# Strassen's scheme for the first product of the last two token chunks of a dense MLP

## The chip, the core and the metric

One core of a Trainium2 chip runs the whole program as one launch. The metric is the device time of one execution, in microseconds. The engines are TensorE (PE, matmuls), VectorE (DVE), ScalarE (ACT), GpSimd (POOL) and SyncE (SP, whose queue issues nearly all transfers). Each engine takes its instructions in the order in which they stand on it.

## What is computed

The program is a chain of three stages on 4 batches of 544 tokens: local attention with global tokens, a gated MLP with a convolution, and this last stage, with its input `x` of 2176 x 512:

```
X = fft over tokens, then over features, real part
u = x + X
un = (u - mean) / sqrt(var + 1e-6)          over the 512 features
out = u + relu(un @ w_ch1) @ w_ch2          w_ch1: 512 x 2048, w_ch2: 2048 x 512
```

All products are made to nearly float32 accuracy: each operand is split in a high and a low part, and `mm3` issues three matmuls (low x high, high x low, high x high) for each 128 x 128 block of weights.

## The kernel before

Features lie on the 128 partitions, tokens on the free axis. The last stage works on five chunks of tokens (`NT = 436`, the last has 432); a chunk's `u` is kept in device memory (`u_d`) and fetched by `load_uc(c)` (L940) into `uc`, as four blocks of 128 features. `ln(c)` (L949) is a generator that makes mean and variance in small steps: VectorE or GpSimd adds the feature blocks, the sum is split in two parts (`sr`), two matmuls with `ones` give the mean in a PSUM bank (L968), VectorE subtracts it (L971), and the centred chunk is stored as high and low parts `chl`. The variance follows in the same way (L987), and its reciprocal root `rs` scales the result at the end.

The hidden layer has 16 blocks of 128. A step `v` of the loop at L1103 stands for one pair (chunk, block): `c_g1(v)` (L998) issues 12 matmuls of `ch1[m]` on `chl` into a bank (`g1` or `pv`), ScalarE takes the relu as the high part and VectorE the low part (`hd`, L1011, L1012), and two steps later `c_g2(v-2)` (L1022) issues 12 matmuls of `ch2[m]` on `hd` into four banks `a0` to `a3`. `plan` (L995) holds 80 steps: chunks 0 and 1 take blocks 0 to 7 and then 8 to 15, then chunks 2, 3 and 4 take all 16 blocks each. So steps 24 to 31 are chunk 1 on blocks 8 to 15, steps 32 to 47 are chunk 2, 48 to 63 chunk 3, and 64 to 79 chunk 4. At a chunk's end VectorE multiplies by `rs` (L1044), adds `uc` (L1047), and SP sends four pieces to `out` (L1049). The last two steps are interleaved by feature block, and the last block is cut in halves (L1032 to L1038).

The weights come as 64-bit floats. `make_c` (L931) turns a block into float32 and splits it, with two value buffers `mags` that are used in turn; blocks 8 to 15 are made by `make_c` in steps 9 to 16 of the program, and some blocks are made earlier, stored in device memory as `kept` and loaded back. PE and SP run strictly in the order of the program text (`manual_schedule`); the order on VectorE, ScalarE and GpSimd is set by a scheduler from priorities. At step 26 the program issues `load_uc(2)`, and at step 27 it starts `ln(2)`, whose mean is due on PE ahead of the first matmuls of step 30:

```
if v in (26, 36, 52):
    load_uc({26: 2, 36: 3, 52: 4}[v])
if v in (1, 27, 36, 52):
    lnq.append(ln({1: 1, 27: 2, 36: 3, 52: 4}[v]))
step(lnq)
c_g1(v)
c_g2(v - 2)
```

Of the kernel before, what the change touches and what calls it, by code (L numbers as in the profile page):

```python
# [151 lines left out]
def fused_kernel(ctx: ExitStack, tc: tile.TileContext, d, out):  # L152
    nc = tc.nc
    pe, act, dve, gp, sp = nc.tensor, nc.scalar, nc.vector, nc.gpsimd, nc.sync
# [780 lines left out]
    ln_t, uc_t, rs_t, cft = {}, {}, {}, []  # L935

    def width(c):
        return min(NT, B * S - NT * c)

    def load_uc(c):  # L940
        t = uc_t[c] = up.tile([128, 5, NT], F32, tag="u", name="uc")
        a, z = NT * c, NT * c + width(c)
# [72 lines left out]
    def c_mm(v, e, a=0, z=None):  # L1015
# [4 lines left out]
        mm3(acc[e][:, a:z], w[:, 0, f], w[:, 1, f], hd[:, 0, a:z], hd[:, 1, a:z], m in one[:2], m in one[2:] and z in (None, width(c)))  # L1020

    def c_g2(v):  # L1022
        end = len(plan) - 2
# [8 lines left out]
        cuts = [(e, 0, n) for e in range(4)]  # L1032
        if v > end:
            cuts[3:] = [(3, 0, h), (3, h, n)]
        for x in cuts:
            if v > end:
                c_mm(end, *x)
            c_mm(v, *x)  # L1038
        if m == 15 or c < 2 and m == 7:
# [2 lines left out]
            for es in [[x] for x in cuts] if v > end else [cuts]:
                for e, a, z in es:
                    dve.tensor_mul(tmp[:, e, a:z], acc[e][:, a:z], rs_t[c][:, a:z])  # L1044
                for e, a, z in es:
                    o = uc[:, e, a:z]
                    dve.tensor_add(o, o, tmp[:, e, a:z])  # L1047
                    if m == 15:
                        sp.dma_start(out[128 * e:128 * e + 128, NT * c + a:NT * c + z], o)  # L1049
# [122 lines left out]
```

## Time and profile before

| | |
|---|---|
| median of three runs | 788.04 us (787.4 to 788.87) |
| the profiled execution | 789.74 us, its span 787.8 us |
| PE busy | 762.4 us, 97% of the span |
| DVE, ACT, POOL busy | 476.9 us, 369.4 us, 167.4 us |
| chain that ended last | PE 78%, DVE 9%, ACT 8%, DMA 2% |

The span runs from the first to the last recorded instruction or transfer of one execution. Steps 0 to 79 of the last stage fill roughly its second half. A busy share is an average over the stages; the chain of waits names, for each moment, the engine on which the end of the program hangs.

### The profile page before, as it was taken

Reading aid. Unit: us, or ns where it says so; the run is one execution under the profiler, and the core shown is the slowest. Engines: PE = TensorE matmul, PEld = TensorE weight load, DVE = VectorE, ACT = ScalarE, POOL = GpSimd, SP = SyncE. Lnnn points to the kernel's source line nnn. Section 1 sums busy time; section 2 is a strip of 40 time slices with the busy share of each in tenths; the row PEclk is TensorE's granted clock in tenths of the full one; section 3 lists DMA queues with packets and bytes.
Section 4 is the critical chain, followed back from the end, with each engine's and each line's share of the span. In section 5 each row is a group of like instructions: output and inputs, shape, how many; then the busy total and the mean of one; then the engine's idle time right before and its main releaser. Section 6 shows DMA issues by size and latency. Waiting matters only on the chain.

```text
span 787.8 us, 13621 instructions
## 1 busy us (share of the span) xinstructions
PE 762.4 (97%) x5278; PEld 701.6 (89%) x5278; DVE 476.9 (61%) x1134; ACT 369.4 (47%) x936; POOL 167.4 (21%) x216
## 2 busy tenths in 40 slices
PE   5898999999999999999999999999999999999997
PEld 4577889998999899998898999999999999999997
DVE  5999977778777878699865778435422132213113
ACT  6988777767777785544442474213131112111110
POOL 3764322323332332000430022100121013000000
PEclk9999999999999999999999999999999999999999
DMA  8754221452337133456430750020200020001001
GB/s 309 268 181 168 85 83 54 162 187 83 102 134 247 56 111 117 112 183 201 146 103 1 275 208 1 1 92 0 92 1 1 1 90 1 1 1 45 1 1 46
DMA packets 37088, 77.80 MB, mean 99 GB/s; under 512 B 3784, under 2 KB 22216, under 8 KB 37024
## 3 DMA queue, kind: packets, MB, share of 16 engines
q1 hardware_dynamic: 36432, 74.52, 27.2%
q0 software_dynamic: 592, 2.42, 1.3%
q8 instruction: 42, 0.69, 0.4%
q14 instruction: 22, 0.18, 0.1%
HBM read 61.72 MB, written 15.20 MB: 98 GB/s over the span
## 4 chain that ended last, share of the span: by engine, by line
PE 78%; DVE 9%; ACT 8%; DMA 2%; issue 1%; POOL 0%; SPq 0%; DVEq 0%; ACTq 0%; POOLq 0%
PE ps_a L169 33%; PE ps_g L169 21%; PE ps_pv L169 15%; PE ps_s L169 5%; PE ps_t L169 3%; ACT pb L346 3%; DVE y L561 1%; DVE mag L659 1%; DVE pb L336 1%; DMA raw_w<-in_w_out_dram 1%; DMA mask<-in_mask_dram 1%; DVE w_w L676 1%; DVE mag L664 1%; ACT h L544 1%; DVE g L581 1%
## 5 line engine op out<-in xcount | busy, mean ns | idle before, releaser
L169 PE MATMUL ps_a<-g,w_w 128*128 128x254 f32 (+1 forms) x768 | 113.5, 295 | 1.3 <-DVE g L581 0.9
L169 PE MATMUL ps_g<-x,w_w 128*128 128x256 f32 (+1 forms) x768 | 111.4, 294 | 3.3 <-ACT h L544 2.1
L169 PEld LDWEIGHTS ps_g<-x,w_w 128*128 128x128 f32 x768 | 100.2, 188 | 10.0 <-ACT h L544 3.7
L169 PEld LDWEIGHTS ps_a<-g,w_w 128*128 128x128 f32 x768 | 101.0, 190 | 6.2 <-issue 3.8
L359 POOL TENSOR_SCALAR pb<-pb,sm 128x224 f32<-128x224 f32 x128 | 85.6, 685 | 83.2 <-DVE sm L354 80.0
L169 PE MATMUL ps_a<-hd,w_w 128*128 128x436 f32 (+1 forms) x480 | 101.4, 360 | 0.0
L169 PEld LDWEIGHTS ps_a<-hd,w_w 128*128 128x128 f32 x480 | 90.1, 188 | 4.8
L561 DVE SCALAR_TENSOR_TENSOR y<-h,convw,y 128x254 f32<-128x254 f32 (+1 forms) x128 | 69.1, 541 | 16.3 <-ACT y L557 15.3
L1012 DVE SCALAR_TENSOR_TENSOR hd<-ps_pv,hd 128x436 fp32r<-128x436 f32 (+1 forms) x40 | 24.2, 604 | 86.9 <-ACT hd L1011 86.9
L169 PE MATMUL ps_a<-hd,w_v 128*128 128x436 f32 (+1 forms) x360 | 76.2, 360 | 0.0
L1011 ACT ACTIVATE hd<-ps_pv 128x436 fp32r<-128x436 f32 (+1 forms) x40 | 21.4, 534 | 111.3 <-PE ps_pv L169 111.3
L1012 DVE SCALAR_TENSOR_TENSOR hd<-ps_g,hd 128x436 fp32r<-128x436 f32 (+1 forms) x40 | 24.3, 607 | 81.2 <-ACT hd L1011 81.2
L1011 ACT ACTIVATE hd<-ps_g 128x436 fp32r<-128x436 f32 (+1 forms) x40 | 21.4, 535 | 110.3 <-PE ps_g L169 110.3
L191 POOL TENSOR_SCALAR mag<-mag 128x512 f32<-128x512 f32 x32 | 26.9, 840 | 208.5 <-ACT mag L190 208.4
L169 PEld LDWEIGHTS ps_a<-hd,w_v 128*128 128x128 f32 x360 | 67.6, 188 | 3.7
L346 ACT ACTIVATE pb<-pb,sm 128x224 f32<-128x224 f32 x128 | 60.4, 473 | 10.7 <-DVE sm L336 10.4
L169 PE MATMUL ps_g<-chl,w_w 128*128 128x436 f32 (+1 forms) x240 | 51.0, 361 | 0.0
L169 PE MATMUL ps_pv<-chl,w_v 128*128 128x436 f32 (+1 forms) x240 | 50.9, 360 | 0.0
L169 PE MATMUL ps_pv<-chl,w_w 128*128 128x436 f32 (+1 forms) x240 | 50.7, 360 | 0.0
L169 PEld LDWEIGHTS ps_pv<-chl,w_v 128*128 128x128 f32 x240 | 45.1, 188 | 2.5
L169 PEld LDWEIGHTS ps_g<-chl,w_w 128*128 128x128 f32 x240 | 44.8, 188 | 2.7 <-issue 0.3
L169 PEld LDWEIGHTS ps_pv<-chl,w_w 128*128 128x128 f32 x240 | 44.9, 188 | 2.5
(224 smaller groups left out, 1388.7 us busy)
## 6 DMA issues: line engine op xcount, KB each, us to landing
v<-in_v_dram SPq DMA_DIRECT2D x16, 640.0 KB, 4.9
qk<-in_qk_dram SPq DMA_DIRECT2D x16, 464.0 KB, 4.8
raw_r<-in_ch_dram SPq DMA_DIRECT2D x14, 512.0 KB, 5.9
raw_v<-in_ch_dram SPq DMA_DIRECT2D x13, 512.0 KB, 9.1
kept<-w_o SPq DMA_DIRECT2D x12, 512.0 KB, 3.5
w_w<-kept SPq DMA_DIRECT2D x12, 512.0 KB, 4.0
qk<-in_qk_dram SPq DMA_DIRECT2D x16, 304.0 KB, 6.1
u_d<-u SPq DMA_DIRECT2D x4, 1088.0 KB, 5.2
```

Source lines behind the costliest of these rows:

```text
L169: return pe.matmul(o, a, b, start=start, stop=stop)
L191: (clamp or dve).tensor_scalar(mag, mag, TOP, 2.0, op0=ALU.min, op1=ALU.max)
L336: dve.tensor_tensor_reduce(out=pb_of(i, k), in0=sb[k // 2][:, k % 2], in1=mask[:, 2 * where(i)[1] + k % 2], scale=-0.125, scalar=3.0e38, o ...
L346: last_exp[0] = act.activation(p, p, AF.Exp, bias=sm[:, k:k + 1], scale=-1.0, accum_out=sm[:, 4 + k:5 + k])
L359: gp.tensor_scalar(pb_of(i, k), pb_of(i, k), sm[:, 12 + k:13 + k], 1.0, op0=ALU.mult, op1=ALU.mult)
L544: act.activation(hbuf[u % NHB][:, h0:h0 + n], h_bank.pop(u), AF.Relu, scale=0.5)
L561: dve.scalar_tensor_tensor(y, o, convw2[:, m, x:x + 1], y, op0=ALU.mult, op1=ALU.add)
L581: dve.tensor_sub(gate[u][:, 1], y, f32(gate[u][:, 0]))
L659: dve.scalar_tensor_tensor(val, val, 3, tail, op0=ALU.logical_shift_left, op1=ALU.bitwise_or)
L664: dve.scalar_tensor_tensor(val, head, -(2**31), val, op0=ALU.bitwise_and, op1=ALU.bitwise_or)
L1011: act.activation(hd[:, 0], o, AF.Relu)
L1012: dve.scalar_tensor_tensor(hd[:, 1], o, 0.0, f32(hd[:, 0]), op0=ALU.max, op1=ALU.subtract)
```

## The change

Chunks 3 and 4 become 434 tokens wide each and are treated as the two columns of a 2 x 2 block product. For `q` from 0 to 7, the rows are blocks `q` and `q + 8` of `w_ch1`, and the inner dimension is cut in two halves of 256 features. Seven products, in the variant with common sums, replace eight: `a11 b11`, `s2 t2`, `s1 t1`, `s3 t3`, `a12 b21`, `s4 b22`, `a22 t4` (`pair`, L1182 of the changed file). A product is 6 matmuls (two slices of 128 features, three each). VectorE adds the products up in SBUF; block `q` and block `q + 8` of chunk 3 go on to the second product at once, the 16 blocks of chunk 4 (`late`) are kept and get their second product at the end.

The sums of the weights (`s1` to `s4`) are made by `s_make(q)` in steps 17, 19, ... 31: VectorE forms them in the two buffers `mags`, SP stores both in device memory (`sval`), and the next `s_make` may overwrite them when the stores have landed. Eight blocks `ch1[8]` to `ch1[15]` are stored as `kept` in steps 9 to 16. In `pair`, `s_load(q + 1)` fetches the sums into `mags` and the plain weights into `aw`, and `s_split` splits the sums into slots `w0` and `w1`. The sums of the activations (`t1` to `t4`) and all seven operands are made in `pair_norm`, a generator on VectorE and ScalarE in steps 36 to 47, normalized before the product; the operands take the slots of `ch1[2]` to `ch1[15]`. The other steps of the program, with their order on PE, are as before.

```diff
--- before.py
+++ after.py
...
 NT = 436
+WIDE = [436, 436, 436, 434, 434]
...
     def width(c):
...
+        return WIDE[c]
...
-    plan += [(c, m) for c in range(2, 5) for m in range(16)]
+    plan += [(2, m) for m in range(16)]
...
     def c_g2(v):
...
-        h = n // 2
-        cuts = [(e, 0, n) for e in range(4)]
-        if v > end:
-            cuts[3:] = [(3, 0, h), (3, h, n)]
-        for x in cuts:
-            if v > end:
-                c_mm(end, *x)
-            c_mm(v, *x)
+        for e in range(4):
+            c_mm(v, e)
...
+    def s_make(q):
+        v0, v1 = mags
+        for v, w in ((v0, ch1[q]), (v1, ch1[q + 8])):
+            dve.tensor_add(v, f32(w[:, 0]), f32(w[:, 1]))
+        a11, a12, a21, a22 = [x[:, y:y + 256] for x in (v0, v1) for y in (0, 256)]
+        dve.tensor_add(a22, a21, a22)
+        dve.tensor_sub(a21, a11, a21)
+        dve.tensor_sub(a11, a22, a11)
+        dve.tensor_sub(a12, a12, a11)
+        for k in range(2):
+            sval[q, k] = dram.tile([128, 512], F32, name=f"sval{q}_{k}")
+            sp.dma_start(sval[q, k], (v0, v1)[k])
+
+    def s_load(q):
+        if q < 8:
+            for k in range(2):
+                sp.dma_start(mags[k], sval[q, k])
+            t = up.tile([128, 3, 512], F32R, tag="u", name="aw")
+            sp.dma_start(f32(t[:, 0:2]), kept[q])
+            sp.dma_start(f32(t[:, 2]).rearrange("p (a b) -> p a b", a=2), kept[q + 8][:, :, 256:512])
+            a_hl[q] = t
+
+    @prio("cv")
+    def s_split(q):
+        if q < 8:
+            s_hl[q] = [put(wp, f"w{k}", mags[k]) for k in range(2)]
...
+    def pair_norm():
+        x = xp.tile([128, 8, NW], F32, tag="x", name="xx")
+        two["x"] = [x[:, 4 * j:4 * j + 4] for j in range(2)]
+        for j in range(2):
+            load_uc(3 + j, two["x"][j])
+        yield
+        yield
+        two["sr"] = up.tile([128, 5, NT], F32R, tag="u", name="xsr")[:, 0:2, 0:NW]
+        x_sum(0)
...
+        t_split("t4", b11)
...
+    def out_add(c, e, o, a=0, z=NW):
+        u = uc_t[c][:, e, a:z]
+        dve.tensor_add(u, u, o)
+        t0 = sum(WIDE[:c])
+        sp.dma_start(out[128 * e:128 * e + 128, t0 + a:t0 + z], u)
...
+        for q in range(8):
+            s_load(q + 1)
+            aw, (s24, s13) = a_hl.pop(q), s_hl.pop(q)
+            wa = {"a11": aw[:, 0:2, 0:256], "a12": aw[:, 0:2, 256:512], "a22": aw[:, 2].rearrange("p (a b) -> p a b", a=2)}
+            for s_, nm in ((s24, "s2 s4"), (s13, "s3 s1")):
+                for k, n_ in enumerate(nm.split()):
+                    wa[n_] = s_[:, :, 256 * k:256 * k + 256]
+
+            def prod(w, x):
+                o = bank(next(four))[:, 0:NW]
+                for k in range(2):
+                    f = slice(128 * k, 128 * k + 128)
+                    mm3(o, wa[w][:, 0, f], wa[w][:, 1, f], t_hl[x][k][:, 0], t_hl[x][k][:, 1], k == 0, k == 1)
+                return o
+
+            x = prod("a11", "b11")
+            with pri("cev"):
+                act.copy(p1, x)
+            if q == 0:
+                c_g2(len(plan) - 1)
+            x = prod("s2", "t2")
+            with pri("cev"):
+                dve.tensor_add(u2, p1, x)
+            x = prod("s1", "t1")
+            with pri("cev"):
+                dve.tensor_add(w5, u2, x)
+            x = prod("s3", "t3")
+            with pri("cev"):
+                dve.tensor_add(late[q + 8], w5, x)
+                dve.tensor_add(u2, u2, x)
+            if q:
+                g2(accs, q + 7, hds.pop(q + 7))
+            x = prod("a12", "b21")
+            with pri("cev"):
+                dve.tensor_add(p1, p1, x)
+            high_low(q, p1)
+            x = prod("s4", "b22")
+            with pri("cev"):
+                dve.tensor_add(late[q], w5, x)
+            s_split(q + 1)
+            x = prod("a22", "t4")
+            with pri("cev"):
+                dve.tensor_add(c21, u2, x)
+            high_low(q + 8, c21)
+            g2(accs, q, hds.pop(q))
+            if q in (5, 7):
+                load_uc(3 if q == 5 else 4)
+        order = [x for q in range(8) for x in (q, q + 8)]
+        high_low(0, late[0])
+        g2(accs, 15, hds.pop(15))
+        for e in range(4):
+            out_add(3, e, accs[e])
+        accs = [bank(next(four))[:, 0:NW] for _ in range(4)]
+        high_low(8, late[8])
+        for k, m in enumerate(order[:14]):
+            if k + 2 < 16:
+                high_low(order[k + 2], late[order[k + 2]])
+            g2(accs, m, hds.pop(m))
+        for e in range(4):
+            for m in order[14:]:
+                g2(accs, m, hds[m], [e])
+            out_add(4, e, accs[e])
...
-        if v in (26, 36, 52):
-            load_uc({26: 2, 36: 3, 52: 4}[v])
-        if v in (1, 27, 36, 52):
-            lnq.append(ln({1: 1, 27: 2, 36: 3, 52: 4}[v]))
+        if 9 <= v < 17:
+            x = TAIL[2 * v - 18]
+            kept[x] = dram.tile([128, 2, 512], F32, name=f"kept{x}")
+            sp.dma_start(kept[x], f32(ch1[x]))
+        if 17 <= v < 33 and v % 2:
+            s_make((v - 17) // 2)
+        if v == 26:
+            load_uc(2)
+        if v in (1, 27):
+            lnq.append(ln({1: 1, 27: 2}[v]))
+        if v == 32:
+            T_SLOTS += [(wp, f"w{m}") for m in range(2, 8)] + [(vp, f"v{m}") for m in range(8, 15)] + [(rb, "r1")]
+            lnq.append(pair_norm())
+        if v == 44:
+            s_load(0)
+        if v == 46:
+            s_split(0)
         step(lnq)
         c_g1(v)
         c_g2(v - 2)
+    c_g2(len(plan) - 2)
+    while lnq:
+        step(lnq)
+    pair()
...
```

Three places in the order of instructions. On SP, at step 25 (end of chunk 0), before:

```order
L205 DMA raw_r_5640<-in_ch_dram 128x1024
L205 DMA raw_r_5642<-in_ch_dram 128x4x256
L205 DMA raw_o<-in_ch_dram 128x1024
L1049 DMA out_dram<-uc 128x436 x4
L946 DMA uc<-u_d_4977 128x4x216
L946 DMA uc<-u_d_5215 128x4x220
```

And now (`mag_5101`, `mag_5102` are the two value buffers; each pair of `sval` rows is one `s_make`, and the first two pairs here are the fourth and the fifth):

```order
L1063 DMA sval_0_6247<-mag_5101 128x512
L1063 DMA sval_1_6249<-mag_5102 128x512
L1063 DMA sval_0_6313<-mag_5101 128x512
L1063 DMA sval_1_6315<-mag_5102 128x512
L1045 DMA out_dram<-uc 128x436 x4
L950 DMA uc<-u_d_4977 128x4x216
L950 DMA uc<-u_d_5215 128x4x220
L1063 DMA sval_0_6398<-mag_5101 128x512
L1063 DMA sval_1_6400<-mag_5102 128x512
```

Between the last load of raw weights and the four stores of chunk 0's result there now stand the stores of eight weight blocks and of five `s_make`s; the two loads of chunk 2's `uc` are behind all of them.

On VectorE, where `ln(2)` makes its sum, before (L958 to L961 are the sum, L971 the subtraction of the mean, `hd` rows belong to steps 26, 27, 28 and 29):

```order
L1012 SCALAR_TENSOR_TENSOR hd<-ps_pv,hd 128x436
L1012 SCALAR_TENSOR_TENSOR hd<-ps_g_6331,hd 128x436
L958 TENSOR_TENSOR cf<-uc 128x872
L959 TENSOR_TENSOR cf<-cf 128x436
L961 TENSOR_TENSOR chl<-cf,chl 128x436
L1012 SCALAR_TENSOR_TENSOR hd<-ps_pv,hd 128x436
L1012 SCALAR_TENSOR_TENSOR hd<-ps_g_6387,hd 128x436
L971 TENSOR_TENSOR cf<-uc,ps_t 128x872 x2
```

And now, starting behind the `hd` row of step 29 (L1055 to L1060 are an `s_make`, here the sixth and half of the seventh; L962, L963 and L965 are the same sum of `ln(2)`):

```order
L1055 TENSOR_TENSOR mag_5101<-w_w_4817 128x512
L1055 TENSOR_TENSOR mag_5102<-w_v_5898 128x512
L1057 TENSOR_TENSOR mag_5102<-mag_5102 128x256
L1058 TENSOR_TENSOR mag_5102<-mag_5101,mag_5102 128x256
L1059 TENSOR_TENSOR mag_5101<-mag_5102,mag_5101 128x256
L1060 TENSOR_TENSOR mag_5101<-mag_5101 128x256
L962 TENSOR_TENSOR cf<-uc 128x872
L1055 TENSOR_TENSOR mag_5101<-w_w_4882 128x512
L963 TENSOR_TENSOR cf<-cf 128x436
L1055 TENSOR_TENSOR mag_5102<-w_v_5944 128x512
L1057 TENSOR_TENSOR mag_5102<-mag_5102 128x256
L965 TENSOR_TENSOR chl<-cf,chl 128x436
```

The sum of `ln(2)` stood ahead of the `hd` rows of steps 28 and 29; now it stands behind both, behind the whole sixth `s_make`, and with three operations of the seventh inside it. The fifth `s_make` stands between the `hd` rows of steps 28 and 29.

On VectorE at the end of chunk 2, before:

```order
L1044 TENSOR_TENSOR cf<-ps_a_6570,uc 128x436
L1012 SCALAR_TENSOR_TENSOR hd<-ps_g_7011,hd 128x436
L1044 TENSOR_TENSOR cf<-ps_a_6571,uc 128x436
L1047 TENSOR_TENSOR uc<-uc,cf 128x436
L1044 TENSOR_TENSOR cf<-ps_a_6572,uc 128x436
L1044 TENSOR_TENSOR cf<-ps_a_6573,uc 128x436
L1047 TENSOR_TENSOR uc<-uc,cf 128x436 x3
```

And now, from the last of chunk 2's adds on (L1227 to L1244 add up the first seven products, L228 are the splits of the next weight sums, L1200 makes the low parts of the first two hidden blocks):

```order
L1043 TENSOR_TENSOR uc<-uc,cf 128x436
L1227 TENSOR_TENSOR hh<-hh,ps_g_7220 128x434
L1230 TENSOR_TENSOR hh<-hh,ps_pv 128x434
L1231 TENSOR_TENSOR hh<-hh,ps_pv 128x434
L228 TENSOR_TENSOR w_w_7259<-mag_5102,w_w_7259 128x512
L1236 TENSOR_TENSOR hh<-hh,ps_s 128x434
L1240 TENSOR_TENSOR hh<-hh,ps_t 128x434
L228 TENSOR_TENSOR w_w_7256<-mag_5101,w_w_7256 128x512
L1244 TENSOR_TENSOR hh<-hh,ps_g_7262 128x434
L1200 SCALAR_TENSOR_TENSOR hd<-hh,hd 128x434 x2
```

For `q = 0` the low part of the first hidden block stands behind the sum of the seventh product; for `q` from 1 to 7 it stands ahead of it.

## Rows read from the trace of the kernel before

**Rows 1.** The page: busy time by engine; granted clock in 40 slices.

```profile
PE 762.4 (97%) x5278; PEld 701.6 (89%) x5278; DVE 476.9 (61%) x1134; ACT 369.4 (47%) x936; POOL 167.4 (21%) x216
...
PEclk9999999999999999999999999999999999999999
```

**Rows 2.** Chain of waits, steps 51 and 77: start us, length us, what.

```profile
640.25 2.38 PE ps_g L169 x12
...
764.23 2.35 PE ps_g L169 x12
```

**Rows 3.** Timeline at the end: start us, length us, engine, instructions.

```profile
781.74 0.48 PE L169 MATMUL ps_a<-hd,w_r 128*128 128x216 f32 x3
...
783.26 0.67 DVE L1044 TENSOR_TENSOR cf<-ps_a,uc 128x216 f32<-128x216 f32 x2
783.85 0.67 DVE L1047 TENSOR_TENSOR uc<-uc,cf 128x216 f32<-128x216 f32 x2
```

**Rows 4.** DMA issues: KB each, median us to landing.

```profile
kept<-w_o SPq DMA_DIRECT2D x12, 512.0 KB, 3.5
w_w<-kept SPq DMA_DIRECT2D x12, 512.0 KB, 4.0
out_dram<-uc SPq DMA_DIRECT2D x16, 218.0 KB, 2.0
out_dram<-uc SPq DMA_DIRECT2D x2, 108.0 KB, 1.7
```

**Rows 5.** Chain of waits, steps 27 to 30.

```profile
526.76 2.37 PE ps_a L169 x12
...
531.52 2.37 PE ps_a L169 x12
...
536.28 2.39 PE ps_a L169 x12
538.67 0.40 PE ps_t L169 x2
```

**Rows 6.** Timelines of DVE and of SP's queue around the end of chunk 0.

```profile
504.06 0.68 DVE L227 TENSOR_TENSOR w_o<-mag,w_o 128x512 fp32r<-128x512 f32 x1
...
520.04 2.94 SPq L1049 DMA_DIRECT2D out_dram<-uc  x4
525.24 1.20 SPq L946 DMA_DIRECT2D uc<-u_d  x2
527.36 0.61 DVE L1012 SCALAR_TENSOR_TENSOR hd<-ps_g,hd 128x436 fp32r<-128x436 f32 x1 [4.16 <-ACT hd L1011]
531.86 1.07 DVE L958 TENSOR_TENSOR cf<-uc 128x872 f32<-128x872 f32 x1 [3.89 <-DMA uc<-u_d]
534.20 0.61 DVE L961 TENSOR_TENSOR chl<-cf,chl 128x436 fp32r<-128x436 f32 x1 [0.62 <-ACT chl L960]
```

**Rows 7.** Groups on DVE by shape: busy us, mean ns.

```profile
L227 DVE TENSOR_TENSOR w_v<-mag,w_v 128x512 fp32r<-128x512 f32 x13 | 9.0, 691 | 6.0 <-ACT w_v L226 6.0
L873 DVE TENSOR_TENSOR ab<-ps_t,ab 92x256 fp32r<-92x256 f32 x5 | 2.1, 419 | 3.6 <-ACT ab L872 3.6
L1047 DVE TENSOR_TENSOR uc<-uc,cf 128x436 f32<-128x436 f32 x24 | 13.7, 604 | 0.0
```

**Rows 8.** Windows after the last matmul: us, five busy times, granted clock, DMA.

```profile
785.00:786.00 1.00, 0.00 (x0) 0.00 (x0) 0.00 (x0) 0.00 (x0) 0.00 (x0) 0.90 0.65 220
786.00:787.00 1.00, 0.00 (x0) 0.00 (x0) 0.00 (x0) 0.00 (x0) 0.00 (x0) 0.50 0.01 2
```

**Rows 9.** Timeline of PE near the start: transposes of one shape, 128 x 128.

```profile
12.84 0.42 PE L375 MATMUL ps_a<-ident,pb 128*128 128x128 f32 x1
13.05 0.42 PE L376 MATMUL ps_a<-ident,pb 128*128 128x128 f32 x1
...
17.91 0.27 PE L375 MATMUL ps_s<-ident,pb 128*128 128x128 f32 x1
18.02 0.27 PE L376 MATMUL ps_s<-ident,pb 128*128 128x128 f32 x1
```

More of the change, by code (lines that the diff above doesn't have):

```diff
@@ L937, in width, with load_uc @@
     def width(c):
[L938 to L942, printed above, removed]
+        return WIDE[c]
+    def load_uc(c, dst=None):
+        if dst is None:
+            uc_t[c] = up.tile([128, 5, NT], F32, tag="u", name="uc")
+            dst = uc_t[c][:, 0:4]
+        a0 = a = sum(WIDE[:c])
+        z = a0 + width(c)
         while a < z:
@@ L945, in load_uc @@
             n = min(z - a, S - o)
-            sp.dma_start(t[:, 0:4, a - NT * c:a - NT * c + n], u_d[b][:, :, o:o + n])
+            sp.dma_start(dst[:, :, a - a0:a - a0 + n], u_d[b][:, :, o:o + n])
             a += n
@@ L1013, in c_g1, with c_mm @@
         hid[v] = hd
-    def c_mm(v, e, a=0, z=None):
+    def c_mm(v, e):
         c, m = plan[v]
@@ L1019, in c_mm @@
         f = slice(128 * e, 128 * e + 128)
-        mm3(acc[e][:, a:z], w[:, 0, f], w[:, 1, f], hd[:, 0, a:z], hd[:, 1, a:z], m in one[:2], m in one[2:] and z in (None, width(c)))
+        mm3(acc[e], w[:, 0, f], w[:, 1, f], hd[:, 0], hd[:, 1], m in one[:2], m in one[2:])
     def c_g2(v):
-        end = len(plan) - 2
-        if not 0 <= v < len(plan) or v == end:
+        if not 0 <= v < len(plan):
             return
@@ L1041, in c_g2 @@
             tmp = cft[0][:, 0:4, 0:n]
[L1042 to L1049, printed above, removed]
+            for e in range(4):
+                dve.tensor_mul(tmp[:, e], acc[e], rs_t[c])
@@ new lines, in c_g2 @@
+            for e in range(4):
+                o = uc[:, e, 0:n]
+                dve.tensor_add(o, o, tmp[:, e])
+                if m == 15:
+                    sp.dma_start(out[128 * e:128 * e + 128, NT * c:NT * c + n], o)
+    NW = WIDE[3]
+    T_SLOTS = []
+    T_ORDER = ("b11", "b21", "t2", "t1", "t3", "b22", "t4")
+    sval, two, t_hl, s_hl, a_hl = {}, {}, {}, {}, {}
+    def s_make(q):
[10 more added lines that the diff above has]
+            sp.dma_start(sval[q, k], (v0, v1)[k])
@@ new lines, in s_load, with x_sum @@
+    def s_load(q):
[10 more added lines that the diff above has]
+            s_hl[q] = [put(wp, f"w{k}", mags[k]) for k in range(2)]
+    def x_sum(j):
+        cf = cft[0]
+        x, sr = two["x"][j], two["sr"]
+        dve.tensor_add(cf[:, 0:2, 0:NW], x[:, 0:2], x[:, 2:4])
+        dve.tensor_add(cf[:, 0, 0:NW], cf[:, 0, 0:NW], cf[:, 1, 0:NW])
+        act.copy(sr[:, 0], cf[:, 0, 0:NW])
+        dve.tensor_sub(sr[:, 1], cf[:, 0, 0:NW], f32(sr[:, 0]))
@@ new lines, in x_mean, with x_center, x_square @@
+    def x_mean(o):
+        sr = two["sr"]
+        mm(o, ones, sr[:, 1], True, False)
+        mm(o, ones, sr[:, 0], False, True)
+        return o
+    def x_center(j):
+        mu = x_mean(fbank()[:, 0:NW])
+        for k in (slice(0, 2), slice(2, 4)):
+            x = two["x"][j][:, k]
+            dve.tensor_sub(x, x, mu[:, None, :].to_broadcast([128, 2, NW]))
+    def x_square(j):
+        cf, sr = cft[0], two["sr"]
+        for k in (slice(0, 2), slice(2, 4)):
+            act.activation(cf[:, k, 0:NW], two["x"][j][:, k], AF.Square)
+        dve.tensor_add(cf[:, 0:2, 0:NW], cf[:, 0:2, 0:NW], cf[:, 2:4, 0:NW])
+        dve.tensor_add(cf[:, 0, 0:NW], cf[:, 0, 0:NW], cf[:, 1, 0:NW])
+        act.copy(sr[:, 0], cf[:, 0, 0:NW])
+        dve.tensor_sub(sr[:, 1], cf[:, 0, 0:NW], f32(sr[:, 0]))
@@ new lines, in x_scale, with t_split @@
+    def x_scale(j):
+        va = x_mean(fbank()[:, 0:NW])
+        rs = cft[0][:, 4, 0:NW]
+        act.activation(rs, va, AF.Sqrt, bias=eps)
+        dve.reciprocal(rs, rs)
+        for k in (slice(0, 2), slice(2, 4)):
+            x = two["x"][j][:, k]
+            dve.tensor_mul(x, x, rs[:, None, :].to_broadcast([128, 2, NW]))
+    def t_split(name, val):
+        i = T_ORDER.index(name)
+        t_hl[name] = []
+        for k in range(2):
+            pool, tag = T_SLOTS[2 * i + k]
+            t = pool.tile([128, 2, NW], F32R, tag=tag, name="t_" + tag)
+            act.copy(t[:, 0], val[:, k])
+            dve.tensor_sub(t[:, 1], val[:, k], f32(t[:, 0]))
+            t_hl[name].append(t)
@@ new lines, in pair_norm @@
+    def pair_norm():
[7 more added lines that the diff above has]
+        x_sum(0)
+        yield
+        yield
+        x_center(0)
+        x_sum(1)
+        yield
+        x_center(1)
+        x_square(0)
+        yield
+        yield
+        x_scale(0)
+        x_square(1)
+        yield
+        b11, b21, b12, b22 = [two["x"][j][:, k:k + 2] for j in range(2) for k in (0, 2)]
+        t_split("b11", b11)
+        yield
+        x_scale(1)
+        cf = cft[0]
+        t1, t2 = cf[:, 0:2, 0:NW], cf[:, 2:4, 0:NW]
+        dve.tensor_sub(t1, b12, b11)
+        dve.tensor_sub(t2, b22, t1)
+        t_split("b21", b21)
+        yield
+        t_split("t2", t2)
+        dve.tensor_sub(b12, b22, b12)
+        yield
+        t_split("t1", t1)
+        yield
+        t_split("t3", b12)
+        dve.tensor_sub(b11, b21, t2)
+        yield
+        t_split("b22", b22)
+        yield
+        t_split("t4", b11)
+        yield
@@ L1102, in fused_kernel @@
     vp = None
-    for v in range(len(plan) + 2):
+    for v in range(len(plan)):
         if v < 9:
```

24 lines of the change are left out of this document (added).

## The prediction

> **What bounds the kernel now.** I read the page first. PE is busy for 97% of the span, at a granted clock of 9 tenths or more in every slice [rows 1]; DVE is busy for 61%, ACT for 47%, POOL for 21%. A busy share is a mean over stages, so the chain of waits comes next, and there only the last stage. From step 28 to the last step it runs on PE without a break: 12 matmuls, then the next 12 [rows 2, 5]. So time is saved here by taking matmuls away and lost wherever PE is made to wait. Twelve matmuls of 436 columns take 2.38 us, 198.3 ns each, and of 432 columns 2.35 us, 195.8 ns each [rows 2]; for 434 I take 197 ns. Last I read the timelines of DVE and of SP's queue around the end of chunk 0, since the change adds work to both there [rows 6].
>
> **What is taken away.** A pair of hidden blocks costs the two chunks 4 x 12 = 48 matmuls in the first product; seven products of 6 are 42. Over eight pairs 48 matmuls go, 48 x 197 ns = **9.5 us**, all on the chain. The second product keeps its 384 matmuls, and the mean and variance their 8.
>
> The Trainium skill (TensorE: Matmul & The Clock Gate, "Back-to-back issue gap") gives columns / 2.4 + 2.5 ns for one warm matmul, 183.3 ns at 434 columns. By that the saving would be 8.8 us and the time 0.7 us longer; the rows are 14 ns above the rule, and the rows decide.
>
> **The tail.** The last feature block is no longer halved. The half matmuls [rows 3] stream the same columns as the whole ones, so that is priced at nothing. Behind the last matmul come four half operations, 783.26 to 784.52, 1.26 us [rows 3], where one add of 0.60 [rows 7] now stands; the last store takes 2.0 where the half one took 1.7 [rows 4]: 0.66 - 0.3, **0.4 us** less.
>
> **What the added work does to step 30.** This decides. The mean of chunk 2 is due on PE at 538.67, ahead of step 30 [rows 5]. Now its loads were issued at 525.24, as soon as the stores of chunk 0's result had landed, its sum began at 531.86 and was ready at 534.81, 3.9 us early [rows 6]. In the changed program those loads stand on SP behind the stores of the fifth `s_make`, and the sum stands on DVE behind the sixth. When is the fifth done? It can't begin before the value buffers are free of `make_c`, whose last operation is at 504.06 [rows 6], and each `s_make` waits for the stores of the one before.
>
> - One `s_make` is two adds of 512 (0.69) and four of 256, each on the result of the one before (0.42, from a row of that width, [rows 7]): 3.1 us. Its two stores, 256 KB each, are nearest to the stores of 218 KB, 2.0 us [rows 4]; with 512 KB it was 3.5. Say 2.4 for both. Five of these chains from 505 take 5 x 3.1 + 4 x 2.4 = 25.1 us without any other work, to 530. But DVE takes its instructions in order, and the `hd` rows and the 8 operations of chunk 0's end stand between: the fifth `s_make` stands behind the `hd` row of step 28. That row begins 0.60 us behind its 12 matmuls (step 27: matmuls end at 526.76, `hd` at 527.36 [rows 5, 6]) and lasts 0.61: 531.52 + 1.21 = 532.7. With 3.1 us, and about 0.4 for the store it may still wait for, the fifth is done at 536.2.
> - SP then issues two stores and four stores of chunk 0, 0.34 us each, the last at 537.9; their data is ready by about 524, and they must land before the buffer can be loaded again, 2.0 us and some queueing: loads at about 540.2 instead of 525.24.
> - From load to sum it took 6.6 us (525.24 to 531.86 [rows 6]): 546.8.
> - The sum took 2.95 us (531.86 to 534.81); three operations of the seventh `s_make` now stand in it, two of 0.6 and one of 0.42, partly beside ScalarE's copy: 4.1 us, ready at 550.9.
>
> PE stands still from 538.67 to 550.9, **12.2 us**. Nothing covers it: PE's next matmuls, step 30, stand behind the mean in the same queue, and after it everything else waits on PE. A floor that needs no transfer time at all: the sum stands behind the `hd` row of step 29 (536.28 + 1.21 = 537.5), the sixth `s_make` (3.1) and itself (4.1), 544.7, so 6.0 us. A ceiling: stores of 3.5 us in each of the last two turns and loads slowed by the stores behind them, 16 us.
>
> **The clock behind that wait.** The last matmuls are over when DVE starts at 783.26 [rows 3]; in the window from 785 the granted clock is 0.90, in that from 786 it is 0.50, the half level of 1.2 GHz [rows 8]. A pause of 12 us should therefore end at half speed. How long PE then stays there is not seen in this part of the trace. Near the start the transposes stand 0.21 us apart at 12.84 and 0.11 us apart at 17.91 [rows 9], so PE ran at half speed for at least these 5 us; half of them, 2.5 us, was lost, and at most about 3, since it had begun a little earlier. Below stands nothing. I take **2.0**: step 30 is denser than that stretch.
>
> **The start of the products.** In steps 36 to 47 DVE makes the operands, and chunk 2's last 8 operations stand between them and the sums of the products. The low part of the first hidden block stands on DVE behind the sum of the seventh product; PE, right behind the seventh product, wants it for its second matmul. Sum 0.6 and low part 0.6 [rows 7], minus one matmul of 0.2: at least 1.0 us; with the split of 0.69 ahead of them and a few tenths of backlog, 2.2. I take **1.6**. From `q = 1` on the low part comes ahead of that sum: behind the fifth product DVE adds (0.6), ScalarE takes the relu, DVE adds the sixth product (0.6) and makes the low part (0.6), 2.4 us with the relu's 0.6 (matmul end to the start of `hd`, 526.76 to 527.36 [rows 5, 6]); PE has 12 matmuls, 2.37 us, and the first of the second product, 0.2, before it wants it. That is free by 0.1 to 0.2 us, and priced at nothing. DVE has 11 operations in a `q`, 6.9 us, against 66 matmuls, 13.0 us, so it is not the bound there. The loads of a `q`, 1.3 MB, have some 6 us each where 512 KB took 4.0 [rows 4]: they lie beside the matmuls, and cost the excess if they don't.
>
> **The sum.** -9.5 - 0.4 + 12.2 + 2.0 + 1.6 = **+5.9 us**. The profiled execution has 789.74 us with a span of 787.8, so 795.6; the median of the runs is 1.7 us lower, 788.04, and I give the time against it: **793.9 us**. What a measurement here can tell from no change is 0.2%, 1.6 us: 786.5 to 789.6 is the same.
>
> **The rivals.**
>
> *The wait is short* and the kernel is faster. Its place is the same, the mean of chunk 2; its price is what is left of 12.2 us if the transfers cost nothing, 6.0, and then the clock has little reason to fall far: -9.9 + 1.6 + 6.0 + 0 to 1 on 788.0, 786. With no wait at all, 779.7. It decides at a wait and clock of 6.7 us together, below which the kernel is faster by more than 0.2%. For it: every engine but PE has room, and the mean was 3.9 us early [rows 6]. Against it: DVE's order alone holds the sum back to 544.7, and SP's order puts the loads behind the fifth `s_make`. The Trainium skill (PSUM — Partial Sum Buffer, "Engine vs sequencer instructions") says that matmuls start and complete in program order, so step 30 can't slip past the mean; no row before shows a matmul that is held up there. Chance 0.14.
>
> *The products are bound by DVE's order.* The margin of 0.1 us per `q` is thin. If each hidden block comes 1 us late, 7 to 14 us are added: 801 to 808. For it: each such add waits for its place on DVE and for ScalarE in turn. Against it: DVE is idle for half of each `q`. Chance 0.09.
>
> *The change doesn't do what it says.* The order shows 42 matmuls in a `q` where 48 stood, so the gain is there; I give this nothing.
>
> **How the numbers follow.** The forecast, a wait of 8 to 16 us at step 30 with the clock behind it, has 0.77; its own range is 787 (wait 8, clock 0, start 1) to 799.5 (16, 3, 2.2). Its low end, a wait of 8 to 9 us with little lost to the clock, is within 0.2% of no change: 0.10 of the 0.77. Of the first rival's 0.14, 0.13 is faster and 0.01 the same. So faster 0.13, same 0.11, slower 0.76 (0.67 and the 0.09 of the second rival). The range 786.5 to 801 leaves out the faster cases and nearly all of the DVE-bound one, about 0.2.
>
> **What would show it.** Right: on the chain one long piece on DMA and DVE between 535 and 555, ending in the sum of `ln(2)`; PE's largest idle time there, its releaser that sum; chunk 0's `out` stores issued some 16 us later than chunk 0's last add; a granted clock of 0.5 in the window behind it; 48 fewer matmuls in `pair`. Wrong: PE busy through 538 to 551, a stall of a microsecond or more in every `q`, or `s_make`s done well before 530.

## The result, and the profile after

| | before | changed |
|---|---|---|
| median (4 runs each, same chip) | 788.45 us | 795.57 us (794.37 to 797.56) |
| ratio, 95% interval | | 1.0094 [1.0069, 1.0118] |
| span of the profiled execution | 787.8 us | 793.7 us |

The kernel is 7.1 us slower by the medians; 793.9 was predicted. From the page of the changed kernel, to set beside [rows 1]:

```profile
PE 756.6 (95%) x5224; PEld 693.7 (87%) x5224; DVE 557.4 (70%) x1274; ACT 386.9 (49%) x970; POOL 146.2 (18%) x204
...
PEclk9999999999999999999999999996999999999999
```

54 matmuls fewer stand there: 48 of the product, and 6 by the tail, where half blocks no longer make two out of one. One slice of 40 has a granted clock of 6 tenths. Its place is named by PE's waits in the second half (time in all, times, longest):

```profile
PE ps_t L170 <- DVE chl L965: 12.3, 1, 12.3
PE ps_a L170 <- DVE hd L1200: 0.8, 1, 0.8
```

The first is the mean of chunk 2 ahead of step 30, the second the start of the products. The chain of waits of the changed kernel around step 30 (start us, length us, what), where [rows 5] showed matmuls alone:

```profile
526.47 1.29 DVE mag L1055 x2
...
529.99 2.59 DMA sval<-mag
532.60 0.70 DVE mag L1055
...
534.71 0.44 DVE mag L1060
535.16 0.32 SPq L1063
...
537.49 2.72 DMA out_dram<-uc
540.23 0.54 SPq L950
540.81 4.82 DMA uc<-u_d
545.72 0.62 DVE cf L962
...
548.97 0.54 DVE chl L965
549.55 1.09 PE ps_t L170 x2
550.65 4.20 PE ps_pv L170 x12
554.85 2.35 PE ps_a L170 x12
```

Read it downwards: the fourth `s_make`, its store, the fifth `s_make`, SP's issue of its two stores and of chunk 0's four stores, their landing, the loads of chunk 2, its sum, the mean. Chunk 0's last add was over at 521.9, and its stores were issued from 536.0 on. PE stands still from 537.26 to 549.55. Then the mean takes 1.09 us where 0.40 is usual, and 12 matmuls 4.20 where 2.38 is. Windows of the changed kernel there (five busy times, granted clock, DMA), to set beside [rows 8]:

```profile
538.00:540.00 2.00, 0.00 (x0) 0.00 (x0) 1.88 (x4) 0.00 (x0) 0.00 (x0) 1.00 0.87 323
540.00:542.00 2.00, 0.00 (x0) 0.00 (x0) 0.43 (x1) 0.00 (x0) 0.00 (x0) 0.72 0.19 27
542.00:554.00 12.00, 4.45 (x12) 4.10 (x13) 8.02 (x13) 2.40 (x3) 0.00 (x0) 0.50 0.46 157
554.00:556.00 2.00, 2.00 (x10) 1.88 (x10) 2.00 (x3) 1.05 (x2) 0.00 (x0) 0.87 0.00 0
```

The clock falls to the half level while PE stands still, and matmuls run at it until the window from 554.

### The profile page after: what moved, and what is told of

It is laid out like the page before. It is cut to its first block, busy times and chain, and to the rows that moved or that the text cites. A ratio compares the mean times of both kernels' runs of the same rounds, so it can differ in the third digit from the quotient of the medians.

```text
span 793.7 us, 13818 instructions
## 1 busy us (share of the span) xinstructions
PE 756.6 (95%) x5224; PEld 693.7 (87%) x5224; DVE 557.4 (70%) x1274; ACT 386.9 (49%) x970; POOL 146.2 (18%) x204
## 4 chain that ended last, share of the span: by engine, by line
PE 75%; DVE 10%; ACT 9%; DMA 3%; issue 2%; SPq 1%; POOL 0%; ACTq 0%; DVEq 0%
PE ps_a L170 27%; PE ps_g L170 19%; PE ps_pv L170 13%; PE ps_s L170 8%; PE ps_t L170 6%; ACT pb L347 3%; DVE y L562 1%; DMA raw_w<-in_w_out_dram 1%; DVE mag L660 1%; DVE pb L337 1%; ACT mag L643 1%; DVE mag L665 1%; DMA raw_w<-in_w_in_dram 1%; DMA uc<-u_d 1%; ACT h L545 1%
## 5 line engine op out<-in xcount | busy, mean ns | idle before, releaser
L170 PE MATMUL ps_a<-hd,w_w 128*128 128x436 f32 (+1 forms) x384 | 82.5, 363 | 0.8 <-DVE hd L1200 0.8
L170 PEld LDWEIGHTS ps_a<-hd,w_w 128*128 128x128 f32 x384 | 71.5, 188 | 6.8 <-DVE hd L1200 2.5
L170 PE MATMUL ps_s<-qk 64*128 64x224 f32 (+1 forms) x144 | 36.3, 404 | 6.0 <-DMA qk<-in_qk_dram 3.7
L567 ACT ACTIVATE y<-y 128x254 f32<-128x254 f32 (+1 forms) x64 | 27.4, 428 | 29.1 <-DVE y L562 29.1
L1200 DVE SCALAR_TENSOR_TENSOR hd<-hh,hd 128x434 fp32r<-128x434 f32 x32 | 19.4, 609 | 27.3 <-ACT hd L1199 27.3
L170 PE MATMUL ps_t<-qk 64*128 64x224 f32 (+1 forms) x144 | 35.7, 398 | 0.0
L577 DVE SCALAR_TENSOR_TENSOR y<-y,h 128x254 f32<-128x254 f32 (+1 forms) x64 | 28.3, 442 | 10.1 <-ACT y L567 9.8
L582 DVE TENSOR_TENSOR g<-y,g 128x254 fp32r<-128x254 f32 (+1 forms) x64 | 28.6, 447 | 9.4 <-ACT g L580 9.4
L545 ACT ACTIVATE h<-ps_g 128x256 f32<-128x256 f32 (+1 forms) x64 | 25.1, 393 | 20.1 <-PE ps_g L170 20.0
L558 ACT ACTIVATE y<-h,convw 128x254 f32<-128x254 f32 (+1 forms) x64 | 33.5, 523 | 2.1 <-DVE g L582 1.5
```

The source lines that it names most:

```text
L170: return pe.matmul(o, a, b, start=start, stop=stop)
L545: act.activation(hbuf[u % NHB][:, h0:h0 + n], h_bank.pop(u), AF.Relu, scale=0.5)
L558: act.mul(y, hb[:, cc:cc + n], convw2[:, m, 1:2])
L567: act.activation(g_t[u], g_t[u], AF.Tanh, scale=0.5)
L577: dve.scalar_tensor_tensor(y, y, 1.0, hbuf[u % NHB][:, cc:cc + n], op0=ALU.add, op1=ALU.mult)
L582: dve.tensor_sub(gate[u][:, 1], y, f32(gate[u][:, 0]))
```

## The experiments

The theory: the change wins some 9 us in the products and loses 15 at one place, the wait and the clock behind it; and the place is a matter of order, on SP and on VectorE. The rivals: the products themselves lose, or the added transfers are too much wherever they stand. Ratios below are to the kernel before on the same chip.

**`makes`: the added work without the products.** The kernel before, with

```diff
+        if 9 <= v < 17:
+            sp.dma_start(kept[x], f32(ch1[x]))
+        if 17 <= v < 33 and v % 2:
+            s_make((v - 17) // 2)
```

> The kernel before, with the change's eight `s_make`s and its eight `kept` stores put at the same steps, and nothing else of the change; what they write is used by nothing, and the products are as before. Theory (the loss of the change is the wait of chunk 2's mean behind the `s_make`s and their stores): PE stands still at step 30 for about 12.3 us as in the changed kernel, and the matmuls behind it run at half the clock for about 2.5 us more, so 788.4 + 14.8 = 803.2 us, between 801 and 805. Rival (the `s_make`s lie beside other work and the loss sits in the products): 788 to 790 us, with PE busy through step 30.

Measured: 803.25 us, ratio 1.0182 [1.0168, 1.0196], 14.6 us slower than before. PE's only wait in that half of the program:

```profile
PE ps_t L169 <- DVE chl L961: 12.4, 1, 12.4
```

So the whole loss comes with the `s_make`s and the eight `kept` stores, and what the rest of the change does is worth 7.1 - 14.6 = -7.5 us. The `kept` stores are not the cause: in `poolq` below they stay on SP, and the loss is gone.

**`late`: the `s_make`s later.**

```diff
-        if 17 <= v < 33 and v % 2:
-            s_make((v - 17) // 2)
+        if 33 <= v < 41:
+            s_make(v - 33)
```

> The changed kernel, with the eight `s_make`s at steps 33 to 40, one a step, in place of the odd steps 17 to 31, so that chunk 2's loads and sum stand in front of all but the first two of them. Theory: the wait of 12.3 us at step 30 and the 2.5 us of slow clock behind it go, and nothing comes in their place, since DVE has room in steps 33 to 40: 795.6 - 14.8 = 780.8 us, between 779.5 and 782.5, a ratio to before of about 0.990; that is 9.9 us of products and tail won, about 1.1 us lost at the start of the products and some 1 us in `pair`. Rival (the work has to stand somewhere, and a second wait comes where it now stands: the centring of chunk 2 before step 32, or the operands of the products at step 47): a gap on PE of several us there, 784 us or more.

Measured: 782.14 us, ratio 0.9915 [0.9902, 0.9927]. The wait at step 30 is gone and the granted clock is 1.00 throughout. PE's waits:

```profile
PE ps_t L170 <- DVE xsr L1085: 1.2, 1, 1.2
PE ps_a L170 <- DVE hd L1200: 0.6, 1, 0.6
PE ps_s L170 <- DVE xsr L1085: 0.4, 1, 0.4
```

Two small new ones have come, for the sums of chunks 3 and 4, whose loads now stand on SP behind stores of the later `s_make`s. That is the rival's mechanism, at a small part of the price that it had. The same work at another place makes the change a gain of 6.5 us.

**`late_q0`: the start of the products, first try.** As `late`, with `s_split(1)` written behind the seventh product.

```diff
-            s_split(q + 1)
+            if q:
+                s_split(q + 1)
             x = prod("a22", "t4")
...
+            if not q:
+                s_split(1)
```

> The kernel `late`, and at the first pair of blocks the split of the next pair's sums (`s_split(1)`) is written behind the seventh product and its relu, not ahead of it, so that it no longer stands on ScalarE and DVE in front of the first hidden block. Theory (PE's gap of 0.8 us at the first matmuls of the second product, and of 1.1 us by the start of the next matmul, is the low part of the first hidden block standing behind that split): 1.0 to 1.2 us less than `late`, about 779.7 us, and the gap is gone from PE's waits. Rival (the gap is DVE's backlog from chunk 2's last eight operations): the gap stays at 0.5 us or more, and the time within 0.4 us of `late`.

Measured: 782.03 us, ratio 0.9914 [0.99, 0.9927], and the wait stays at 0.6 us. ScalarE's timeline says why:

```profile
639.83 0.62 ACT L227 CAST w_w<-mag 128x512 fp32r<-128x512 f32 x1 [1.77 <-PE ps_t L170]
640.36 0.56 ACT L1199 ACTIVATE hd<-hh 128x434 fp32r<-128x434 f32 x1
```

The split still stands ahead of the relu of the first hidden block: the order on ScalarE is the scheduler's, and moving the text did not move it. The run fits the rival's number, but it tells nothing on the cause; `poolq_q0` below does.

**`fill` and `fill62`: the clock alone.** In the changed kernel, 50 (62) matmuls ahead of the mean:

```diff
+        if c == 2:
+            for k in range(50):
+                mm(mu, ch1[15][:, 0, 0:128], ch1[15][:, 0, 0:n], True, True)
```

> The changed kernel, with 50 matmuls of 436 columns ahead of the mean of chunk 2, into the bank that the mean then overwrites; their result is used by nothing. At 198 ns they fill 9.9 us of the 12.3 us in which PE stands still. Theory (the 1.09 us of the mean and the 4.20 us of the 12 matmuls behind it, where 0.40 and 2.38 are usual, come from the clock that falls in the pause): the granted clock stays at 1.00, the two pieces take 0.4 and 2.4 us, and the time is 2.5 us less than the changed kernel, 793.1 us; PE's wait for the sum is 2.4 us in place of 12.3. Rival (those pieces are long because their operands come late, or because of the loads and stores beside them): they stay long, and the time is 795.6 us.

Measured: 794.12 us, ratio 1.0069 [1.0054, 1.0084], between both numbers. PE's timeline, and windows behind the 50 matmuls:

```profile
536.73 9.83 PE L170 MATMUL ps_t<-w_r 128*128 128x436 f32 x50
549.40 1.09 PE L170 MATMUL ps_t<-chl,ones 128*128 128x436 f32 x2 [2.84 <-DVE chl L965]
550.29 3.63 PE L170 MATMUL ps_pv<-chl,w_v 128*128 128x436 f32 x12
```

```profile
548.00:549.00 1.00, 0.00 (x0) 0.00 (x0) 0.96 (x3) 0.35 (x1) 0.00 (x0) 1.00 0.00 0
549.00:550.00 1.00, 0.60 (x2) 0.57 (x3) 0.97 (x3) 0.00 (x0) 0.00 (x0) 0.62 0.00 0
550.00:551.00 1.00, 1.00 (x4) 0.92 (x3) 0.96 (x3) 0.00 (x0) 0.00 (x0) 0.50 0.00 0
```

The theory's expectation was wrong in one thing: the 2.8 us of pause that were left were enough. The clock fell in the window from 549, in which PE starts again, so the mean and most of the 12 matmuls behind it ran at the half level.

> As `fill`, with 62 matmuls in place of 50: 12.3 us, nearly the whole of the pause, where `fill` left 2.8 us of it and still had a clock of 0.50 in the windows from 550 to 552 and a piece of 3.43 us for the 12 matmuls behind it. Theory (the clock falls after any pause of that size, and is worth 0.7 + 1.8 = 2.5 us here): PE's wait for the sum is under 0.5 us, the clock stays at 1.00, the two pieces take 0.4 and 2.4 us, and the time is 793.1 us. Rival (the matmuls of step 30 are slow for another reason, the transfers beside them): they stay at 3 us or more, and the time is that of `fill`, 794.1, or above.

Measured: 792.71 us, ratio 1.0059 [1.0038, 1.0079]. PE waits 0.5 us, the clock stays at 1.00, and 12 matmuls take their usual time:

```profile
548.83 0.67 PE L170 MATMUL ps_t<-chl,ones 128*128 128x436 f32 x2 [0.47 <-DVE chl L965]
549.34 2.55 PE L170 MATMUL ps_pv<-chl,w_v 128*128 128x436 f32 x12
```

The mean takes 0.67 us behind this short wait at full clock too, so of the 1.09 only 0.42 is the clock's. Its share is (1.09 - 0.67) + (4.20 - 2.38) = 2.2 us by the chain of the changed kernel, and 795.57 - 792.71 = 2.9 us by the medians. The intervals of the two runs overlap, so the medians alone would not show it. The traces agree with the chain: from the variance of chunk 1 (436.63 in the changed kernel, 435.76 here) to the end of the last matmul (789.67, 786.73) `fill62` is 2.1 us shorter. Transfers are no cause: in the windows of `fill` from 549 to 551 there are none (DMA share 0.00), and the clock is low.

**`poolq`: another queue for sixteen stores.** In the changed kernel:

```diff
-            sp.dma_start(sval[q, k], (v0, v1)[k])
+            gp.dma_start(sval[q, k], (v0, v1)[k])
```

> The changed kernel with one thing changed: the sixteen stores of the `s_make`s are issued from POOL's queue, not SP's. The `s_make`s stay on DVE at the same steps. This takes away SP's order (chunk 0's stores and chunk 2's loads behind the fifth `s_make`'s stores) and leaves DVE's order: the sum of chunk 2 still stands behind the fifth `s_make` and the `hd` row of step 29, and the first add of the sixth stands inside it. Theory (both orders take part, DVE's alone some 4 of the 12.3 us: sum begun at about 537, ready at 541 to 543 against a mean due at 537.3): PE's wait 3.5 to 6 us, the clock behind it 1.8 to 2.5 us, 785.5 to 789 us, 787 in the middle. Rival 1 (SP's order is all of it): no wait, 781 us. Rival 2 (DVE's order is all of it): 795.6 us.

Measured: 779.95 us, ratio 0.9894 [0.9875, 0.9912], faster than the 785.5 to 789 that was expected; no wait at step 30. SP's and VectorE's timelines there, to set beside [rows 6]:

```profile
518.66 3.98 SPq L1045 DMA_DIRECT2D out_dram<-uc  x4
524.57 2.25 SPq L950 DMA_DIRECT2D uc<-u_d  x2
```

```profile
526.17 0.42 DVE L1060 TENSOR_TENSOR mag<-mag 128x256 f32<-128x256 f32 x1
531.83 1.07 DVE L962 TENSOR_TENSOR cf<-uc 128x872 f32<-128x872 f32 x1 [5.24 <-DMA uc<-u_d]
...
535.39 0.60 DVE L965 TENSOR_TENSOR chl<-cf,chl 128x436 fp32r<-128x436 f32 x1
```

Chunk 2's loads go out at 524.57, as before the change. It looks like rival 1, but one thing came with it: the scheduler that orders VectorE, with nothing changed but the queue of the stores, now puts the sum behind the fourth `s_make` (ends 526.6), not the sixth. The late place on VectorE was a consequence of SP's order. So the run doesn't measure VectorE's order; the next one does.

**`poolq_order`: VectorE's order held as in the changed kernel.** As `poolq`, with

```diff
+        if c == 2:
+            tc.add_manual_dep(first.ins, made[5].ins.name, ...)
```

> The kernel `poolq`, with one dependence added: the first add of chunk 2's sum comes behind the last operation of the sixth `s_make`, as it stands on DVE in the changed kernel. In `poolq` the program's planner, with the loads early, had put that sum behind the fourth `s_make`, so `poolq` took away both orders, not SP's alone. Theory (the prediction's floor: DVE's order alone costs 6.0 us whatever the transfers take, and the clock something more): sixth `s_make` done at 538 to 540.5, sum ready at 541.5 to 544 against a mean due at 537.0, so PE waits 4.5 to 7 us, and the clock behind it takes 2 us: 779.95 + 6.5 to 9 = 786.5 to 789 us. Rival (with the loads early the sum's place on DVE costs nothing, since the `s_make`s come faster too): under 1 us of wait, 780 to 781 us.

Measured: 787.98 us, ratio 0.9996 [0.9986, 1.0005]. The chain:

```profile
538.87 0.44 DVE mag L1063
...
542.13 0.54 DVE chl L968
542.71 1.09 PE ps_t L170 x2
543.80 3.98 PE ps_pv L170 x12
```

PE waits 5.6 us (its last matmul ends at 537.1), the mean takes 0.27 more as in `fill62`, and the clock takes (1.09 - 0.67) + (3.98 - 2.38) = 2.0 us; together 7.9, and the medians differ by 8.0. With VectorE's order alone, no difference to the kernel before can be measured: the products' gain and this loss cancel.

**`poolall`: the `s_make`s off VectorE and SP altogether.**

```diff
     def s_make(q):
-            dve.tensor_add(v, f32(w[:, 0]), f32(w[:, 1]))
+            gp.tensor_add(v, f32(w[:, 0]), f32(w[:, 1]))
...
-            sp.dma_start(sval[q, k], (v0, v1)[k])
+            gp.dma_start(sval[q, k], (v0, v1)[k])
```

> The changed kernel with the `s_make`s as a whole (their six operations and their two stores) on POOL, at the same steps; POOL is idle in that stretch. Neither DVE nor SP then has any of this work in front of chunk 2's sum. Theory (the cost of the added work is its place in DVE's and SP's order, and not the transfers or the memory): no wait at step 30, the clock stays at 1.00, 795.6 - 14.8 = 780.8 us, between 779.5 and 782.5. Rival (POOL's operations are longer, or hold up DVE's while both work, or the value loads at step 44 come before the last stores are down): a wait at another place, 784 us or more.

Measured: 779.62 us, ratio 0.9886 [0.9867, 0.9905]. PE's only wait left in that half is the 0.8 us at the start of the products. The transfers are the same in number and size, so it is the place of the added work that costs.

**`best`: an order by hand.**

```diff
-        if 17 <= v < 33 and v % 2:
-            s_make((v - 17) // 2)
+        for q, at in enumerate((17, 19, 21, 33, 34, 35, 36, 37)):
+            if v == at:
+                s_make(q)
...
+            norm = pair_norm()
+            next(norm)
```

> The changed kernel with the `s_make`s at steps 17, 19, 21 and 33 to 37, and the loads of the pair's chunks issued at step 32, ahead of the later stores, not behind `ln(2)`. In `late` PE waited 1.2 and 0.4 us for the sums of these two chunks, whose loads were issued at 576.75, behind the stores. Theory: that wait goes and the first three `s_make`s are done before chunk 2's sum, so 1.6 us less than `late`: 780.5 us, and of PE's waits only the 0.6 to 0.8 us at the start of the products stays. Rival (the third `s_make`, at 515 to 523, holds up chunk 0's end and with it chunk 2's loads, or the fourth stands in front of the sum): a wait at step 30 of some us, 783 us or more.

Measured: 782.08 us, ratio 0.9915 [0.9897, 0.9932], no better than `late`. The two waits of `late` are gone, and one has come at step 30:

```profile
PE ps_t L170 <- DVE chl L965: 1.2, 1, 1.2
```

This is the rival's place, at a smaller price: chunk 2's loads stand behind the third `s_make`'s stores.

**`poolq_q0`: the start of the products, held by a dependence.** As `poolq`, with the split's two copies and two subtractions behind the relu and the low part of the first hidden block:

```diff
-            s_split(q + 1)
+            s_split(q + 1, (relu[0], low[0]) if q == 0 else None)
```

> The kernel `poolq`, with the two copies of the split of the second pair's sums put by a dependence behind the relu of the first hidden block, and its two subtractions behind that block's low part. `late_q0` meant the same and left the order on ScalarE and DVE as it was. Theory (that split in front of the first hidden block is what PE waits for at the start of the products, 0.8 us by the waits, 1.1 us by the start of the next matmul): the wait is gone or under 0.3 us, and the time is 0.6 to 1.1 us less than `poolq`, about 779.1. Rival (chunk 2's last eight operations on DVE are behind it too): 0.4 us or more of the wait stays.

Measured: 779.61 us, ratio 0.9883 [0.9861, 0.9905]. No wait of PE is listed in that half any more, and the first 12 matmuls of the second product begin on time:

```profile
640.49 2.63 PE L170 MATMUL ps_a<-hd,w_w 128*128 128x434 f32 x12
```

That the split was what PE waited for is shown by the trace: chunk 2's eight operations still stand ahead, so the rival is out. The piece is still about 0.1 us longer than the others, as it is in every later `q` (below). The medians don't tell: 0.3 us less than `poolq`, with intervals that overlap. The two traces do: from the first product's first matmul to the end of the last matmul it is 627.27 to 774.54 in `poolq` and 629.77 to 775.71 here, 1.3 us less.

## Why the prediction was right

| term | predicted, us | measured, us | from |
|---|---|---|---|
| products, 48 matmuls | -9.5 | -9.5 | 6 matmuls in 1.19, 198 ns each |
| tail | -0.4 | -0.55 | below |
| wait at step 30 | +12.2 | +12.3 | waits; 12.4 in `makes` |
| clock behind it | +2.0 | +2.1 to 2.9 | chain 2.2; `fill62` |
| mean behind a wait | 0 | +0.3 | 0.67 for 0.40, `fill62` |
| start of the products | +1.6 | +1.4 | below |
| second product, `q` >= 1 | 0 | about +0.8 | below |
| sum | +5.9 | +6.8 to 7.7 | medians +7.1, spans +5.9 |

**Medians and spans.** In the changed kernel's profile the mean of chunk 2 is due at 537.26, in that of before at 538.67 [rows 5]. That 1.4 us is no work of the change: PE's timelines have it at the variance of chunk 1 already (436.63 and 438.05), ahead of the first added store, which SP issues at 455.66. The profiled execution of before took 789.74 us, 1.3 us over the median of the four runs. Added to the spans' 5.9 the 1.4 gives 7.3, near the medians' 7.1.

**The wait** came about as laid out, step by step; that it was met to 0.1 us is luck. On the clock of the profile before, 1.4 us later, the fifth `s_make` was done at 536.5 (536.2 predicted), the loads were issued at 541.6 (540.2), the sum began at 547.1 (546.8) and was ready at 550.9 (550.9). Two misses cancel. From the `s_make` to the loads it took 5.1 us and not 4.0: the issue of a store of chunk 0 took 0.45 us, where 0.34 had been put without a row for it, and they landed in 2.7, not 2.0. From the loads to the sum it took 5.5 us and not 6.6. The floor of 6.0 us by VectorE's order, which was an argument only, was measured as 5.6 in `poolq_order`. What the argument lacked is that this order is no fact of its own: free SP, and the scheduler moves the sum.

**The clock** was the term of the first rival that failed. With a wait of 6 us it was given 0 to 1 us, "the clock has little reason to fall far"; `poolq_order` shows 2.0 behind 5.6 us, and `fill` (1.09 - 0.67) + (3.43 - 2.38) = 1.5 behind 2.8 us (3.43 is the piece on its chain). At its own floor that rival would have come out at no change, not faster. The 2.0 of the forecast was near, and so were the 5 us at half speed behind it: PE worked at the half level from 549.55 to about 554.5. But the choice of 2.0 and not 2.5, because step 30 is denser, was tested by no run. And the stretch near the start that gave the 5 us shows half speed by the spacing of its transposes alone; the granted clock printed for its windows is 1.00.

**The start of the products.** PE's timeline of the changed kernel, from the last three matmuls of the seventh product on:

```profile
652.51 0.76 PE L170 MATMUL ps_g<-t_r,aw 128*128 128x434 f32 x3
653.25 0.47 PE L170 MATMUL ps_a<-hd,w_w 128*128 128x434 f32 x1
654.55 2.45 PE L170 MATMUL ps_a<-hd,w_w 128*128 128x434 f32 x11 [0.83 <-DVE hd L1200]
656.84 1.38 PE L170 MATMUL ps_pv<-t_w,aw 128*128 128x434 f32 x6
```

The first matmul of the second product was due at 653.10 and came 0.15 us late; the second, which reads the low part, came another 1.1 us late. The piece ends at 656.84 and not at 653.10 + 2.37 = 655.47, 1.4 us late. The step was right that the split and the sums stand in front of it, and the backlog was a little smaller than assumed.

**The margin of a `q`.** Priced at nothing with 0.1 to 0.2 us free; it is about 0.1 us short. For `q` = 3, PE's timeline of the changed kernel (the second products of blocks `q` + 7 and `q`) and VectorE's:

```profile
688.02 2.52 PE L170 MATMUL ps_a<-hd,w_v 128*128 128x434 f32 x12
...
693.95 2.65 PE L170 MATMUL ps_a<-hd,w_w 128*128 128x434 f32 x12
```

```profile
693.49 0.60 DVE L1200 SCALAR_TENSOR_TENSOR hd<-hh,hd 128x434 fp32r<-128x434 f32 x1
```

The low part is done at 694.09, just when the second matmul of the second piece is due, and that piece is 0.13 us longer than the first. The excess lies in its first two matmuls, 0.67 us where the first piece has 0.55, and the second of them is the first to read the low part. Seven such pieces make the 0.8. That the low part is the cause was not tried on its own. So the second rival had its place right and its price ten times too high, and PE never waited a microsecond there. The loads of a `q` took 3.4 to 4.3 us to land and hold nothing up.

**The tail.** The last matmuls and the last add of the changed kernel (chain):

```profile
788.48 1.20 PE ps_pv L170 x6
...
789.71 0.61 DVE uc L1178
```

From the last matmul's end to the span's end it is 793.7 - 789.68 = 4.0 us; before, 787.8 - 783.23 = 4.6.

**The two rules of the skill.** The Trainium skill (TensorE: Matmul & The Clock Gate, "Back-to-back issue gap") has a formula for a single matmul by itself, from which 183.3 ns is an estimate; the rows after show 198, so the rows were rightly followed. The Trainium skill (PSUM — Partial Sum Buffer, "Engine vs sequencer instructions") has matmuls in program order; the trace agrees: the 12 matmuls of step 30 stood for 12.3 us behind the two of the mean, though they need nothing of chunk 2.

## What to carry to other kernels

A cut in matmuls pays only as far as the work that it calls for finds a place: here 9 us were won and 15 lost, because ten stores, the last of them waiting for a late producer, stood on one queue ahead of the loads of the next chunk. Before judging such a change, follow the queue that it adds to, and ask which load stands behind; issuing the same stores from another queue, one word of the program, turned 0.9% slower into 1.1% faster. An order that one engine shows can come from another queue: the sum's late place on VectorE went when the stores left SP. A pause of PE can cost more than its length: behind pauses of 2.8, 5.6 and 12.3 us, one trace each, the half clock took another 1.5, 2.0 and 2.2 us.

## What was not expected of the hardware

- The price of the clock grew far less than the pause: 1.5 us behind 2.8, and 2.2 behind 12.3. Pauses of 1.2 us (`late`, `best`) left it at 1.00.
- In `poolall`, while POOL does the `s_make`s, VectorE's operations with both operands in SBUF take longer, the adds for the output twice as long in the mean. Groups of VectorE from 500 to 560, `poolq` first, then `poolall` (busy us, mean ns):

```profile
L1043 DVE TENSOR_TENSOR uc<-uc,cf 128x436 f32<-128x436 f32 x7 | 4.1, 602 | 0.0
L1040 DVE TENSOR_TENSOR cf<-ps_a,rs 128x436 f32<-128x436 f32 x4 | 2.3, 604 | 0.1
```

```profile
L1043 DVE TENSOR_TENSOR uc<-uc,cf 128x436 f32<-128x436 f32 x5 | 5.8, 1183 | 0.0
L1040 DVE TENSOR_TENSOR cf<-ps_a,rs 128x436 f32<-128x436 f32 x4 | 2.3, 602 | 4.2 <-PE ps_a L170 4.2
```

Those with one operand in PSUM keep their time. The Trainium skill (GPSIMD Engine Reference, "1. Specifications") says that the two engines share their way to SBUF and get in each other's way where VectorE has two SBUF inputs; the trace agrees. It cost nothing here, since VectorE was not what PE waited for.
